# Spread tables in steps behind the mode products, the first pair's x w behind the last unit, and Y's first rows built pair by pair, in a windowed attention with a Fourier mixing layer

## The chip, the cores and the metric

The kernel runs on one core of one Trainium2 chip. The metric is the device time of one execution in microseconds; 433.08 us is the median of three runs of the kernel before (432.17 to 433.22). Times inside an execution count from the start of the profiled span.

## The reference

Eight batches, eight heads, 576 positions, head width 64. Attention looks back over 64 positions; its output, heads side by side, is x (8 x 576 x 512). Then, over the sequence:

```
X  = rfft(x, axis=1)                     # only the first 64 modes are used
Yr = Xr @ w_r[m] - Xi @ w_i[m]           # per mode m: a 512 x 512 matrix pair
Yi = Xr @ w_i[m] + Xi @ w_r[m]
y  = irfft(Y, n=576);  u = x + y
out = u + relu(u @ w_ch)
```

The 64 modes' two matrices are 128 MiB in float32 and are read once. The kernel splits u @ w_ch into x @ w_ch and y @ w_ch, and computes the latter as (inverse transform) @ (Y @ w_ch).

## The kernel before, in words

**First part (0 to about 190 us).** Attention and forward transform, while GpSimd (POOL) already issues loads of mode matrices, cast to bf16 on the way. Modes are taken in 16 groups of four. The first ten groups (`EARLY`) need their weights in two halves of the input channels: the first halves are used during attention, the second ones right after it.

**Second part.** The loop at L1048 walks over the remaining entries of `steps`. Each entry has two halves, `ri` 0 and 1, which use one load of `w_r` and one of `w_i`, each 1024 KB as it lands. Twenty halves finish the first ten groups with `mode_half` (L198); then 24 halves do the six other groups with `mode_pair` (L216), two modes at a time. One half is: 8 or 16 small matmuls with the weights of one load as the moving operand; `load_weights`, which has POOL issue the next load as soon as a buffer is free; whatever `ready` holds (mostly the turn of the last result by four matmuls, L694 or L722); and some calls of `advance`, paced by `want` (L1096 to L1104). Of `steps[20:]` all loads go to the three buffers of `ringA`, so a load can only be issued once the half that used the buffer's old content has been computed. The instruction order of every engine is the program's order.

`advance` works off a list of jobs with a delay of one: it prepares a job and finishes the one before. The first jobs are x @ w_ch for 36 tiles of 128 rows: four transposes (L639), an ACT copy (L614), four float32 matmuls into a bank (`multiply`, L646), a DVE copy to `XW` (L856). Ten of these (`NX0`) go beside the first twenty halves.

**The boundary** (`i == EARLY`, L1051): the jobs are drained, memory of the first stage is closed, Zall and the second XW pool are opened, part of Yall is cleared, and `spread_tables` (L768) runs. It makes, from the inverse transform's tables `trigI` (bf16) and `trigIr` (float32), copies whose rows are spread to the row order of the last two groups' results (`trigL`, `trigX`, `trigLr`, `trigXr`). For each of the two tables DVE clears a scratch tile and copies identity columns into it (L775, L777), TensorE multiplies (L782, L786, L789: six matmuls), and ACT copies four results out of PSUM (L790 to L792). One table's scratch is a `stg` tile, the other's a `tr` tile. The results are first used behind the loop, at L900 and L907.

**The last units.** Groups 12 and 13 (`LAST`, `LAST + 1`) come last, as four pairs of modes, i = 0 to 3. When group 15 is complete, the batch jobs start: for each batch the first 112 rows of Y are turned, multiplied with `w_ch` (`Zall`), and used for the output tiles (`early_u` L806, `add_late` L796), as many calls of `advance` as the pacing puts behind each of the eight last halves. Before the half before last all jobs are finished. Before the very last half (L1068) three `put_first` (L727; they gather the pairs' results, transposed, as rows of Y into a bank `late["first"]` of pool `z`) and `tail_xw(0)` (L890: XW of the first two output tiles into PSUM) are issued. `tail_xw` uses a float32 identity, `put_first` two matmuls of 256 columns.

**The end** (L1108 on): pair 3's `turn`, `put_first`, `take` (ACT and DVE copies into `trz`, L733); YL copied from `first`, L1115; the last rows' product with `w_ch`, L1119, in a bank of pool `y` and one of pool `z`; then for each pair of output tiles the low-rank products (L900, L907), additions and the store by SP. PSUM has eight banks: pools `m`, `t` and `z` with two each, `y` and `p` with one each. A bank is only written again when its last content has been read.

Of the kernel before, what the change touches and what calls it, by code (L numbers as in the profile page):

```python
# [9 lines left out]
FP32 = mybir.dt.float32  # L10
FP32R = mybir.dt.float32r
# [15 lines left out]
def kernel(  # L27
# [196 lines left out]
    with tc.manual_schedule():  # L224
# [480 lines left out]
        def finish_pair(grp, h, psm):  # L705
            if h == 0:
                late["stg"] = stgpool.tile([128, DM], BF16, name="stg")
            stg = late["stg"][:, HALF * h:HALF * h + HALF]
            nc.vector.tensor_copy(out=stg, in_=psm[:, 0:HALF])
            i = 2 * (grp % 2) + h  # L710
            end = grp - grp % 2 == LAST
            if i == (1 if end else 0):
                late["pt"] = bank("p", [128, NDCH, 128])
            other = bank("m", [128, NDCH, 128]) if end and i == 3 else None

            def pts(half):
                return other if half and other else late["pt"]

            def turn():
                for c in range(NDCH):  # L720
                    half = c // 2
                    nc.tensor.matmul(out=pts(half)[:, c, 32 * i:32 * i + 32], lhsT=stg[:, 128 * (c % 2):128 * (c % 2) + 128],  # L722
                                     rhs=lateT[:, half] if end else sel[:, half::2], start=True, stop=True)

            def put_first():
                for half in range(2):
                    nc.tensor.matmul(out=late["first"][:, HALF * half:HALF * half + HALF],  # L727
                                     lhsT=pick[:, half, 88 - 8 * i:216 - 8 * i], rhs=stg,
                                     start=(i == half == 0), stop=(i == 3), skip_group_check=True)

            def take():
                for by, cs in ((nc.scalar.copy, slice(0, 2)), (nc.vector.tensor_copy, slice(2, 4))):
                    by(out=trz[:, cs, :, 8 * i:8 * i + 8],  # L733
                       in_=pts(cs.start // 2)[:, cs, 32 * i:32 * i + 32].rearrange("p c (g x) -> p c g x", x=8))

            def prepare():
                turn()
                if end:
                    take()
                elif i == 3:  # L740
                    give_rows(grp, late["pt"])

            if end:
                late[i] = turn, put_first, take
            if end and i == 0:
                late["held"] = prepare
            elif not (end and i == 3):
                if end and i == 1:
                    ready.append(late["held"])
                ready.append(prepare)  # L750
# [14 lines left out]

            jobs.append((prepare, done))

        def spread_tables():  # L768
            for table, wide, two, one, spread in (
                    (trigI, trigL, trigX, ident_bf, stgpool.tile([128, DM], BF16, name="stg")),  # L770
                    (trigIr, trigLr, trigXr, ident_r,
                     trpool.tile([128, NDCH, 128], FP32R, name="tr").rearrange("p c k -> p (c k)"))):
                spread = spread[:, 0:256].rearrange("p (x g k y) -> p x g k y", x=2, g=4, y=2)
                plain = spread if table is trigI else spread.bitcast(FP32)
                nc.vector.memset(plain.rearrange("p x g k y -> p (x g k y)"), 0.0)  # L775
                for x in range(2):
                    nc.vector.tensor_copy(out=spread[:, x, :, :, x],  # L777
                                          in_=one[:, rows].unsqueeze(1).to_broadcast([128, 4, 16]))
                pt = bank("y")
                for x in range(2):  # L780
                    lhsT = spread[:, x].rearrange("p g k y -> p (g k y)")
                    nc.tensor.matmul(out=pt[:, 0:128], lhsT=lhsT, rhs=table[:, S - 64 + 64 * x:S + 64 + 64 * x],  # L782
                                     start=(x == 0), stop=(x == 1))
                for x in range(2):
                    lhsT = spread[:, x].rearrange("p g k y -> p (g k y)")
                    nc.tensor.matmul(out=pt[:, 128 + 64 * x:192 + 64 * x], lhsT=lhsT, rhs=table[:, 512:S],  # L786
                                     start=True, stop=True, skip_group_check=True)
                    pw = bank("z")
                    nc.tensor.matmul(out=pw, lhsT=lhsT, rhs=table[:, 0:512], start=True, stop=True)  # L789
                    nc.scalar.copy(out=wide[:, x, 0:512], in_=pw)  # L790
                nc.scalar.copy(out=two, in_=pt[:, 0:128])
                nc.scalar.copy(out=wide[:, :, 512:S], in_=pt[:, 128:256].rearrange("p (x k) -> p x k", x=2))  # L792

        UE = {}

# [187 lines left out]

        def new_ut():
            nonlocal taken_uts
            if not homes:
                homes.append(utpool.tile([128, 2, DM], FP32, name="utx"))
            elif taken_uts == len(homes) < NUT:
                t = ringA.tile([128, 4, DM], FP32, name="ut", tag="wt")
                homes.extend([t[:, 0:2], t[:, 2:4]])  # L990
            taken_uts += 1
            return homes[(taken_uts - 1) % NUT]
# [51 lines left out]
        NX0 = 10  # L1044
        x_jobs(pool("xp0", reuse_waits="tile"), 0, NX0)
        half = given = 0
        n0, n1 = 2 * EARLY, 4 * (NGRP - EARLY)
        for i, (grp, hb) in enumerate(steps[EARLY:]):  # L1048
            if i == 2:
                whole_modes()  # L1050
            if i == EARLY:  # L1051
                while tables:
                    tables.pop(0)()
                while jobs or pend:
                    advance()
                close(stmp2, yp, ringB)
                Zall = pool("zall", side="right").tile([2 * NM, B, DM], FP32R, name="Zall")
                x_jobs(pool("xp1", side="right", reuse_waits="tile"), NX0, NT)
                utpool = pool("utpool", side="right", reuse_waits="tile")
                nc.vector.memset(YT[:, :, :, rows], 0.0)  # L1060
                spread_tables()
                given = 0
            psm = bank("m")
            for ri in range(2):
                if half == n0 + n1 - 2:
                    while jobs or pend:
                        advance()
                if half == n0 + n1 - 1:  # L1068
                    late["first"] = bank("z")
                    for pair in range(3):  # L1070
                        late[pair][1]()
                    tail_xw(0)
                (mode_half if grp < EARLY else mode_pair)(psm, EARLY + i, ri)
                load_weights(len(wlist))
                while ready:
                    ready.pop(0)()
                for t in tables[0:2]:
                    t()
                del tables[0:2]
                if half == 0:  # L1080
                    nc.gpsimd.dma_start(out=wch, in_=moe_w_ch.rearrange("(c p) e -> p c e", p=128))
                if ri:
                    if grp < EARLY:
                        finish_group(grp, psm)
                    else:
                        finish_pair(grp, hb, psm)
                    if (grp, hb) == (NGRP - 1, 1):
                        ready.pop(0)()
                        for b in range(B):
                            batch_job(b)  # L1090
                            if 0 < b <= NLB:
                                early_jobs(b - 1)
                            if b % 2:
                                add_late(9 * (b // 2) + 8)
                half += 1
                if half <= n0:  # L1096
                    want = max(half - 4, 0) * NX0 // (n0 - 4)
                elif half <= n0 + n1 - 8:
                    want = (half - n0) * (NT - NX0) // (n1 - 8)
                else:  # L1100
                    want = NT - NX0 + (half - n0 - n1 + 8) * (B + 7 * NLB + 4) * 2 // 11
                while given < want:
                    advance()
                    given += 1  # L1104
# [2 lines left out]

        turn, put_first, take = late[3]  # L1108
        first = late["first"]
        turn()  # L1110
        put_first()
        ZL = trpool.tile([128, NDCH, 128], FP32R, name="tr").rearrange("p c k -> p (c k)")
        YL = stgpool.tile([128, DM], BF16, name="stg")
        take()
        nc.vector.tensor_copy(out=YL, in_=first)  # L1115
        zl = [bank("y"), bank("z")]
        for h, ps_ in enumerate(zl):
            for c in range(NDCH):
                nc.tensor.matmul(out=ps_[:, 0:HALF], lhsT=trz[:, c].rearrange("p g k -> p (g k)"),  # L1119
# [55 lines left out]
```

## Time and profile before

| | |
|---|---|
| median of three runs | 433.08 us (432.17 to 433.22) |
| the profiled execution | 433.11 us, of which the span is 431.1 us (2.0 us lie around it) |
| TensorE (PE) matmuls | 330.0 us busy, 77% of the span |
| VectorE (DVE) / ScalarE (ACT) / GpSimd (POOL) | 238.6 / 182.9 / 103.8 us |
| DMA | 93.28 MB by the page's count of packets, mean 216 GB/s; HBM read 163.58 MB |
| mean granted TensorE clock | 0.905 |
| the chain that ended last | DMA 55%, PE 28%, issue 7%, DVE 5% |

Busy times of engines overlap, so they do not add up to the span. The chain of waits says which of them set the end: up to 361 us mostly transfers of `w_r` and `w_i`, after that PE with DVE. GB/s in the profile counts what the DMA engines write; a load of 1024 KB at 213 GB/s takes 4.9 us. A timeline line gives start, duration, engine, line, operation, operands, count, and in brackets how long the engine was idle before it and what ended that. PEld is the loading of the stationary operand, which runs beside PE.

### The profile page before, as it was taken

Reading aid. Unit: us, or ns where it says so; the run is one execution under the profiler, and the core shown is the slowest. Engines: PE = TensorE matmul, PEld = TensorE weight load, DVE = VectorE, ACT = ScalarE, POOL = GpSimd, SP = SyncE. Lnnn points to the kernel's source line nnn. Section 1 sums busy time; section 2 is a strip of 40 time slices with the busy share of each in tenths; the row PEclk is TensorE's granted clock in tenths of the full one; section 3 lists DMA queues with packets and bytes.
Section 4 is the critical chain, followed back from the end, with each engine's and each line's share of the span. In section 5 each row is a group of like instructions: output and inputs, shape, how many; then the busy total and the mean of one; then the engine's idle time right before and its main releaser. Section 6 shows DMA issues by size and latency. Waiting matters only on the chain.

```text
span 431.1 us, 11458 instructions
## 1 busy us (share of the span) xinstructions
PE 330.0 (77%) x5006; PEld 218.2 (51%) x5006; DVE 238.6 (55%) x509; ACT 182.9 (42%) x330; POOL 103.8 (24%) x153
## 2 busy tenths in 40 slices
PE   6999999999999999973307344676575668979994
PEld 3666767576677667651104122444453445535552
DVE  7688787877776766866104111123222224874995
ACT  5665757566666656532201101142121213433663
POOL 8322223222131231112112100011111111120894
PEclk8899999999999999988557768569999989999999
DMA  8999999999999999999999999989999999995698
GB/s 203 211 211 212 212 211 212 211 211 212 211 213 211 212 212 211 212 212 212 211 258 212 212 211 212 215 173 212 215 215 214 214 214 214 215 214 113 223 364 310
DMA packets 40819, 93.28 MB, mean 216 GB/s; under 512 B 2529, under 2 KB 2785, under 8 KB 40769
## 3 DMA queue, kind: packets, MB, share of 16 engines
q0 software_dynamic: 35056, 81.80, 98.4%
q1 hardware_dynamic: 5568, 10.62, 6.7%
q8 instruction: 39, 0.64, 0.5%
q10 hardware_dynamic: 144, 0.13, 0.1%
q14 instruction: 12, 0.09, 0.1%
HBM read 163.58 MB, written 9.44 MB: 401 GB/s over the span
## 4 chain that ended last, share of the span: by engine, by line
DMA 55%; PE 28%; issue 7%; DVE 5%; ACT 2%; POOL 2%; DVEq 0%; POOLq 0%
DMA wr<-in_moe_w_r_dram 34%; DMA wi<-in_moe_w_i_dram 12%; DMA rawk<-in_k_dram 7%; PE tr L260 4%; PE s L307 3%; PE psz L646 2%; PE s L319 2%; PE s L299 2%; PE pt L327 2%; PE vb L272 2%; DVE xw L802 2%; PE psm L198 1%; PE psm L216 1%; PE o L347 1%; DMA vd<-in_k_dram 1%
## 5 line engine op out<-in xcount | busy, mean ns | idle before, releaser
L646 PE MATMUL psz<-wch,tr 128*128 128x512 f32 x176 | 59.2, 466 | 11.4 <-DMA wch<-in_moe_w_ch_dram 10.9
L856 DVE CAST xw<-psz 128x512 fp32r<-128x512 f32 x36 | 24.9, 692 | 73.6 <-PE psz L646 73.1
L311 DVE TENSOR_REDUCE mx<-s 128x4 fp32r<-128x512 f32 x72 | 49.5, 688 | 24.2 <-PE s L307 23.9
L614 ACT CAST tr<-ptx 128x512 fp32r<-128x512 bf16 x36 | 21.2, 588 | 95.4 <-PE ptx L639 95.4
L321 ACT ACTIVATE p<-s 128x512 bf16<-128x512 f32 x72 | 39.7, 602 | 13.0 <-PE s L319 13.0
L646 PEld LDWEIGHTS psz<-wch,tr 128*128 128x128 f32 x176 | 35.1, 221 | 18.7 <-issue 11.3
L198 PEld LDWEIGHTS <-XQ 128*32 128x32 bf16 x320 | 13.0, 175 | 45.5 <-issue 27.3
L264 ACT COPY kT<-tr 128x576 bf16<-128x576 bf16 x32 | 23.2, 725 | 22.8 <-PE tr L260 22.8
L198 PE MATMUL psm<-wi,XQ 128*32 128x512 bf16 x144 | 14.8, 486 | 20.6 <-DMA wi<-in_moe_w_i_dram 20.6
L307 PE MATMUL s<-kT,qT 64*64 64x128 bf16 (+1 forms) x576 | 29.2, 221 | 0.0
L299 PE MATMUL s<-mask_t,ident_bf 128*128 128x512 bf16 x72 | 28.4, 395 | 0.6
L330 DVE COPY pts<-pt 128x1024 bf16<-128x1024 bf16 (+1 forms) x40 | 25.2, 630 | 5.3 <-PE pt L327 3.8
L264 ACT COPY qT<-tr 128x576 bf16<-128x576 bf16 x32 | 23.3, 727 | 9.8 <-PE tr L260 9.8
L686 DVE TENSOR_TENSOR stg<-psm,Yfour 128x512 bf16<-128x512 f32 x10 | 6.9, 690 | 36.4 <-PE psm L198 33.5
L178 POOL DMA_DIRECT2D wi<-in_moe_w_i_dram x18 | 13.7, 758 | 55.3 <-PE psm L198 35.5
L307 PEld LDWEIGHTS <-qT 64*64 64x64 bf16 x576 | 18.0, 107 | 17.7 <-issue 17.2
L319 PE MATMUL s<-mx,ident_r 128*128 128x512 f32 x72 | 26.2, 437 | 0.0
L169 POOL DMA_DIRECT2D wr<-in_moe_w_r_dram x12 | 8.4, 698 | 69.8 <-PE psm L216 33.3
L264 ACT COPY vT<-tr 128x576 bf16<-128x576 bf16 x32 | 23.3, 728 | 4.0 <-PE tr L260 3.9
L198 PE MATMUL psm<-wr,XQ 128*32 128x512 bf16 x120 | 11.9, 478 | 16.3 <-DMA wr<-in_moe_w_r_dram 15.7
L327 PE MATMUL pt<-ident_bf,p 128*128 128x128 bf16 x288 | 23.3, 220 | 0.9 <-issue 0.8
L216 PEld LDWEIGHTS <-XQ 128*32 128x32 bf16 x256 | 9.2, 151 | 29.3 <-issue 29.2
(259 smaller groups left out, 672.2 us busy)
## 6 DMA issues: line engine op xcount, KB each, us to landing
wi<-in_moe_w_i_dram POOLq DMA_DIRECT2D x29, 1024.0 KB, 19.1
wr<-in_moe_w_r_dram POOLq DMA_DIRECT2D x27, 1024.0 KB, 19.2
out_dram<-ut SPq DMA_DIRECT2D x29, 256.0 KB, 2.8
rawv<-in_v_dram POOLq DMA_DIRECT2D x16, 288.0 KB, 16.0
rawk<-in_k_dram POOLq DMA_DIRECT2D x15, 288.0 KB, 15.1
rawq<-in_q_dram POOLq DMA_DIRECT2D x15, 288.0 KB, 15.0
x_sb<-in_moe_w_r_dram POOLq DMA_DIRECT2D x2, 1024.0 KB, 15.9
out_dram<-utx SPq DMA_DIRECT2D x6, 256.0 KB, 2.6
```

Source lines behind the costliest of these rows:

```text
L198: nc.tensor.matmul(out=psm[32 * g:32 * g + 32, :], lhsT=XQ[hb].rearrange("k s b m -> k (s b) m")[:, (3 * j + 1 - ri) * B:(3 * j + 5 - ri) ...
L264: nc.scalar.copy(out=to, in_=pt.rearrange("p j n -> p n j"))
L299: nc.tensor.matmul(out=s, lhsT=ident_bf, rhs=mask_t[:, mk], start=True, stop=True)
L307: nc.tensor.matmul(out=s[ro, t, lo:128], lhsT=lq, rhs=kT[ro, 64 * n - 64 + lo:64 * n + 64], start=False, stop=True, skip_group_check=True)
L311: nc.vector.tensor_reduce(out=mx, in_=s, axis=AX.X, op=ALU.max, negate=True)
L319: nc.tensor.matmul(out=s, lhsT=ident_r, rhs=mx.unsqueeze(2).to_broadcast([128, 4, 128]), start=False, stop=True, skip_group_check=True)
L321: nc.scalar.activation(out=p[:, 4 * c2:4 * c2 + 4, :], in_=s, func=ACT_F.Exp, scale=EX_SCALE)
L327: nc.tensor.transpose(out=pt[:, t, :], in_=st[u]["p"][:, t, :], identity=ident_bf)
L330: nc.vector.tensor_copy(out=ps[:, 0:nt, :], in_=pt[:, 0:nt, :])
L614: nc.scalar.copy(out=tr, in_=pt)
L646: nc.tensor.matmul(out=pz, lhsT=tr[:, c, :], rhs=wch[:, c, :], start=(c == 0), stop=(c == NDCH - 1))
L856: nc.vector.tensor_copy(out=XW[i], in_=multiply(tr))
```

## The change

Three things move; nothing is computed that was not computed before.

1. `spread_tables` becomes `spread_steps`, three functions: `clear` (all DVE work of both tables) and one `multiply_by` for each table (its six matmuls and four ACT copies). From the second half behind the boundary on, one of them runs per half, behind the half's products and `ready`. The scratch is the first output tile `utx`, which is now taken at the boundary, and `trz`. The jobs are no longer drained at the boundary, so the tenth x @ w_ch product comes one half later.
2. `put_first` is called inside each pair's `prepare`, behind its `turn`, and its bank comes from pool `y`, taken with pair 1. The two banks of the last rows' product both come from pool `z`.
3. `tail_xw(0)` moves from before the last half to behind the loop, just before pair 3's `turn`.

```diff
             if i == (1 if end else 0):
                 late["pt"] = bank("p", [128, NDCH, 128])
+                if end:
+                    late["first"] = bank("y")
...
                 turn()
                 if end:
+                    put_first()
                     take()
...
-        def spread_tables():
-            for table, wide, two, one, spread in (
...
+        def spread_steps(scratch):
+            flat = scratch.rearrange("p j e -> p (j e)")[:, 0:128]
+            flat_r = trz.rearrange("p c g k -> p (c g k)")[:, 0:256]
+            todo = ((trigI, trigL, trigX, ident_bf, flat.bitcast(BF16), flat),
+                    (trigIr, trigLr, trigXr, ident_r, flat_r, flat_r.bitcast(FP32)))
...
+            def clear():
+                for table, wide, two, one, spread, plain in todo:
+                    nc.vector.memset(plain, 0.0)
+                    for x in range(2):
+                        nc.vector.tensor_copy(out=lanes(spread)[:, x, :, :, x],
+                                              in_=one[:, rows].unsqueeze(1).to_broadcast([128, 4, 16]))
+
+            def multiply_by(table, wide, two, one, spread, plain):
                 pt = bank("y")
...
+            return [clear] + [lambda t=t: multiply_by(*t) for t in todo]
...
-                while jobs or pend:
-                    advance()
                 close(stmp2, yp, ringB)
...
                 nc.vector.memset(YT[:, :, :, rows], 0.0)
-                spread_tables()
+                homes.append(utpool.tile([128, 2, DM], FP32, name="utx"))
+                spread = spread_steps(homes[0])
...
-                if half == n0 + n1 - 1:
-                    late["first"] = bank("z")
-                    for pair in range(3):
-                        late[pair][1]()
-                    tail_xw(0)
                 (mode_half if grp < EARLY else mode_pair)(psm, EARLY + i, ri)
                 load_weights(len(wlist))
                 while ready:
                     ready.pop(0)()
+                if spread and half > n0:
+                    spread.pop(0)()
...
         first = late["first"]
+        tail_xw(0)
         turn()
         put_first()
...
-        zl = [bank("y"), bank("z")]
+        zl = [bank("z"), bank("z")]
```

`n0` is 20, the number of the first stage's halves; `half` counts all of them, 0 to 43.

More of the change, by code (lines that the diff above doesn't have):

```diff
@@ L766, in batch_job, with lanes @@
             jobs.append((prepare, done))
-        def spread_tables():
-            for table, wide, two, one, spread in (
[L770 to L778, printed above, removed]
+        def spread_steps(scratch):
[3 more added lines that the diff above has]
+                    (trigIr, trigLr, trigXr, ident_r, flat_r, flat_r.bitcast(FP32)))
+            def lanes(spread):
+                return spread.rearrange("p (x g k y) -> p x g k y", x=2, g=4, y=2)
+            def clear():
[5 more added lines that the diff above has]
+            def multiply_by(table, wide, two, one, spread, plain):
                 pt = bank("y")
                 for x in range(2):
-                    lhsT = spread[:, x].rearrange("p g k y -> p (g k y)")
+                    lhsT = spread[:, 128 * x:128 * x + 128]
                     nc.tensor.matmul(out=pt[:, 0:128], lhsT=lhsT, rhs=table[:, S - 64 + 64 * x:S + 64 + 64 * x],
@@ L784, in spread_tables @@
                 for x in range(2):
-                    lhsT = spread[:, x].rearrange("p g k y -> p (g k y)")
+                    lhsT = spread[:, 128 * x:128 * x + 128]
                     nc.tensor.matmul(out=pt[:, 128 + 64 * x:192 + 64 * x], lhsT=lhsT, rhs=table[:, 512:S],
@@ L985, in new_ut @@
             nonlocal taken_uts
-            if not homes:
-                homes.append(utpool.tile([128, 2, DM], FP32, name="utx"))
-            elif taken_uts == len(homes) < NUT:
+            if taken_uts == len(homes) < NUT:
                 t = ringA.tile([128, 4, DM], FP32, name="ut", tag="wt")
@@ L1046 @@
         half = given = 0
+        spread = []
         n0, n1 = 2 * EARLY, 4 * (NGRP - EARLY)
```

## The prediction

> **What bounds the kernel now.** I read the chain of waits first. From 243 us it consists of transfers of `w_r` and `w_i` with a 0.7 us group of PE products behind each, until 361.05 us; from there it runs through PE and DVE to the end. So a microsecond won before 361 us counts only if a transfer lands earlier, and one won behind it counts if PE or DVE on that chain gets it. The change touches both parts: the tables at 278 to 288 us, the order around the last unit at 394 to 398 us.
>
> For the first place I read the stretches of two microseconds (columns: window, its length, then busy time and count of PE, PEld, DVE, ACT, POOL, granted clock, DMA share, GB/s):
>
> ```profile
> 284.00:286.00 2.00, 1.14 (x4) 1.14 (x5) 0.00 (x0) 0.81 (x3) 0.00 (x0) 0.50 1.02 205
> 286.00:288.00 2.00, 2.00 (x22) 1.02 (x21) 0.00 (x0) 1.51 (x4) 0.00 (x0) 0.50 0.62 125
> 288.00:290.00 2.00, 2.00 (x28) 1.35 (x28) 0.23 (x1) 1.07 (x2) 0.71 (x1) 0.50 0.63 117
> 290.00:292.00 2.00, 2.00 (x13) 1.55 (x11) 0.59 (x2) 0.69 (x2) 0.70 (x1) 0.79 0.97 172
> 292.00:294.00 2.00, 2.00 (x30) 1.38 (x29) 0.99 (x2) 0.57 (x2) 0.30 (x1) 1.00 1.07 215
> ```
>
> DMA has a hole just behind the tables: against 213 GB/s it lacks 88, 96 and 41 GB/s for 2 us each, 450 KB, worth 450 / 213 = 2.1 us. The timeline shows the cause:
>
> ```profile
> 276.67 1.12 PE L198 MATMUL psm<-wi,XQ 128*32 128x512 bf16 x8 [1.27 <-DMA wi<-in_moe_w_i_dram]
> 278.08 3.26 PE L646 MATMUL psz<-wch,tr 128*128 128x512 f32 x8
> 282.78 0.33 PE L782 MATMUL psy<-trigI,stg 128*128 128x128 bf16 x2 [1.44 <-DVE stg L777]
> 284.86 0.69 PE L782 MATMUL psy<-trigIr,tr 128*128 128x128 f32 x2 [1.26 <-ACT trigL L792]
> 286.86 1.08 PE L216 MATMUL psm<-wr,XQ 128*32 128x256 bf16 x16
> 288.26 0.71 POOL L169 DMA_DIRECT2D wi<-in_moe_w_i_dram  x1 [9.48 <-PE psm L216]
> 296.25 0.67 PE L216 MATMUL psm<-wi,XQ 128*32 128x256 bf16 x16 [1.44 <-DMA wi<-in_moe_w_i_dram]
> 301.94 0.67 PE L216 MATMUL psm<-wr,XQ 128*32 128x256 bf16 x16 [2.49 <-DMA wr<-in_moe_w_r_dram]
> ```
>
> The first L216 starts at 286.86 behind the tables and waits for no DMA; POOL waited 9.48 us for it before it could issue the next load. The trace's completion marks (sixteen per load, one for each DMA engine) give that L216's load as landed at 281.58: it ran 5.3 us late.
>
> **Is the hole on the path?** The second thing to see: products that wait for their load start at 242.06 and, seven loads on, at 276.67, 4.94 us per load; from 276.67 to 296.25 four loads, 4.90 us each. Across the hole no landing is late. The sixteen marks say why. Of the load that landed at 281.58 eight came at 276.4 to 277.5 and eight at 280.7 to 281.6; of the one at 291.31 eight at 286.2 to 287.3 and eight at 290.4 to 291.3; of the one at 296.20 all at 295.4 to 296.2. Eight engines run up to 5 us ahead of the others, and the hole is their idle time. The late eight were busy until 290.4 to 291.3, and the load issued at 288.26 was there for them (296.20 - 291.31 = 4.89, one full pace). Products wait for the last mark, so filling the hole gives the early eight their lead back and moves no landing. The Trainium skill, "DMA: Bandwidth & Descriptors", section "Why a DMA increments its semaphore by 16 and not by 1", says that the engines of one transfer finish independently and only the full count means landed; these marks agree.
>
> **The change, part by part.**
>
> *Tables.* Removed from before the first L216: one product of four matmuls, the tables' twelve matmuls (0.83 us from 282.78 and 2.08 us from 284.86) and their waits for DVE and ACT. L216 can start at its landing, 281.6; POOL issues the next load at about 283.0 instead of 288.26; SP has no issue near. Value by the marks 0; ends 0 and -2.1 (the whole hole as time).
>
> *Where the tables go.* By the instruction order they stand behind the products of the third and fourth half (landings about 291.3 and 296.2). Each adds to its half at most 0.83 or 2.08 us of PE, plus waits for two pool-`z` banks emptied by ACT (1.07 + 0.28 + 0.30 = 1.65 us, and 1.78 us, of ACT); queued behind are only that half's transposes and x @ w_ch products. The cover is PE's wait for loads: 24.0 us in 12 halves from 296 to 356 us, 2.0 each. Value 0. Without cover at most 0.83 + 1.65 + 2.08 + 1.78 = 6.3 us; but L216 was 5.3 us late before without a late landing, so nearly all of that is absorbed even then. `clear` is the same six DVE instructions, DVE idles 7 of 10 there: 0. The job that is no longer drained is one product a half later; the pacing ends in the same state: 0. `utx` and `trz` are not used until 383 us: 0.
>
> *`put_first` pair by pair.* Pairs 0 and 1 give four matmuls to the stretch at 383 us, about 0.1 us each by their weight loads (six in 0.56). Two lie inside PE's wait of 0.56 us for DVE at 383.61. The other two push L815 from 383.71 to about 383.9; the addition L821 stands on DVE behind a copy that ends at 384.36 anyway. Value 0, ends 0 and +0.2. Its bank `y` was last read near 374.7, and the next use of `y` is L900: 0.
>
> *Last unit.* The stretch that sets the end:
>
> ```profile
> 394.45 0.69 PE L216 MATMUL psm<-wr,XL 128*32 128x256 bf16 x16
> 395.06 0.17 PEld L722 LDWEIGHTS <-stg 128*128 128x128 bf16 x4 [0.17 <-issue]
> 395.15 0.56 PEld L727 LDWEIGHTS <-pick 128*128 128x128 bf16 x6
> 395.72 0.30 PEld L890 LDWEIGHTS pst<-xw,ident_r 128*128 128x128 f32 x2
> 396.39 0.69 PE L216 MATMUL psm<-wi,XL 128*32 128x256 bf16 x16
> 397.15 0.42 DVE L709 CAST stg<-psm 128x256 bf16<-128x256 f32 x1 [1.32 <-PE psm L216]
> 397.63 0.21 PE L722 MATMUL psp<-pick,stg 128*128 128x32 bf16 x2 [0.56 <-DVE stg L709]
> ```
>
> Here the chain has PE at 394.45, then the last L216, the cast, the turn. After the change only two of six L727 stand before the last L216: 395.15 + 0.19, then the 0.17 to 0.25 gap that PEld shows before a new group: L216 at 395.55, against 396.39, 0.8 earlier. Its last load has its last mark at 395.30, so 0.25 us of room is left. The cast then ends at 396.75. Meanwhile L890 takes its 0.67 us (395.72 to 396.39) behind L216's weights (395.55 + 0.44): done at 396.8 with a gap of 0.15, at 397.0 with the 0.36 that stands before L216 here. PE was idle 0.56 us in that place. The turn starts at 396.8 to 397.05 instead of 397.63: 0.6 to 0.8 gained, 0.8 taken, because the short gap belongs to bf16 groups before. Behind it the same instructions follow; YL's bank `y` is free once L1115 has read it, where L900 before waited for L663; both `z` banks are read by the same copies: 0 (ends -0.2 and +0.2).
>
> **Sum.** 0 + 0 + 0 - 0.8 on the profiled execution's 433.11 us (span 431.1, 2.0 around it) gives 432.3; that execution lies 0.03 above the median, so the forecast for the median is **432.3**. About 0.3% (1.3 us: 431.8 to 434.4) is what a measurement of this kernel can tell from no change.
>
> **Rivals.**
>
> *The hole is time.* If the early engines' lead is worth something (they take over what delays the late ones), landings move by up to 2.1 us and everything from 296 to 394 us follows, since PE waits for loads up to 361.05. For it: the page's 173 GB/s in that slice. Against: four landings on pace. 433.1 - 2.1 - 0.8 = 430.2, though the last marks must move with it. The Trainium skill's fit for one transfer, in "DMA: Bandwidth & Descriptors", section "Anatomy of one DMA — SWDGE (gpsimd) path", makes time a fixed part plus bytes over a rate; read that way, missing bytes are missing time. The marks speak against that reading.
>
> *One late landing goes.* The load at 301.94 came 5.69 us behind the one before, 0.8 over the pace; fifteen marks came by 301.16, one at 301.90, and a 16 KB packet of queue q8 (0.94 us) ran at 296.48. If after the change an early engine carries this, landings move 0.8: 431.5.
>
> *Nothing on the last unit.* L890 now stands between the last L216 and the turn; if it costs its 0.71 us there in full, or the last load's marks end later, the gain is near 0: 433.0.
>
> *Slower: PE falls behind the loads at the tables.* Place: second to fifth half, 286 to 307 us. The clock was 0.50 from 284 to 290 us; if, with PE now waiting for loads between groups, it stays there, rows of this clock give: second half L216 1.08 + two jobs of 0.61 + 2.06 = 6.4 us, third 1.08 + 0.39 + 0.83 + 2.67 = 5.0, fourth 1.08 + 2.08 + 5.34 = 8.5, fifth 1.08 + 0.39 + 5.34 = 6.8, end to end from 286.5 to 313.2, where the sixth half starts 6.4 us behind its load of 306.8. With all of ACT's 1.65 and 1.78 us as waits it is 9.8. It decides above the 5.3 us that were harmless: 1.1 to 4.5 us of missing landings, 2.8 in the middle, less 0.8: 435.1. Against it: PE is busy without a pause from 286.5 on in this case, and before such a stretch brought the full clock within the window from 290 us (0.79). The Trainium skill, "TensorE: Matmul & The Clock Gate", section "What's actually happening", states that activity releases a halved clock; it would end this rival after some microseconds, as at 290 us.
>
> **How the numbers follow.** Forecast 432.3: 0.49. Hole 430.2: 0.18. One landing 431.5: 0.10. Nothing gained 433.0: 0.10. Slower 435.1: 0.13. Faster by over 0.3%: 0.18 + 0.10 = 0.28. Within: 0.49 + 0.10 = 0.59. Slower: 0.13. The range 430.1 to 434.0 takes in the hole's end and leaves out the slower case; the forecast's own is 431.8 to 432.8.
>
> **What would show it.** After the change: no window under 200 GB/s between 284 and 294 us, the first L216 at about 281.6 and the next load issued near 283; yet the products at about 296.2, 301.9 and 361.0 unmoved. The last L216 at about 1.9 us behind the start of the one before it becomes 1.1; the last turn comes 2.4 us behind it instead of 3.2. If the product at 361.0 comes at 359, the marks misled me; if L216 falls over 5 us behind its landing after 291 us, the slower rival holds.

## The result, and the profile after

| | before | after |
|---|---|---|
| median (executions) | 432.98 us (432.17 to 435.62; 19) | 432.07 us (431.46 to 432.49; 19) |
| profiled execution, its span | 433.11, 431.1 us | 432.25, 430.4 us |
| mean granted TensorE clock | 0.905 | 0.886 |
| DMA and PE in the chain that ended last | 55%, 28% | 49%, 37% |

The ratio after to before is 0.9975 (95% interval 0.9963 to 0.9986), 1.1 us of 433. The forecast was 432.3 us, 0.8 below the profiled execution of before; the profiled execution of after is 0.86 below it. The chain of waits follows loads until 376.24 us now (361.05 before); what comes behind is PE with ACT and DVE, as before.

First the stretches behind the boundary in the kernel after (columns as in the prediction: window, length, busy time and count of PE, PEld, DVE, ACT, POOL, granted clock, DMA share, GB/s):

```profile
284.00:286.00 2.00, 1.20 (x3) 0.53 (x3) 0.76 (x2) 0.07 (x1) 0.00 (x0) 0.50 1.06 213
286.00:288.00 2.00, 1.56 (x21) 1.16 (x21) 1.37 (x7) 0.00 (x0) 0.16 (x1) 0.50 1.07 215
288.00:290.00 2.00, 2.00 (x8) 1.28 (x8) 0.08 (x2) 0.59 (x1) 0.54 (x1) 0.50 1.08 219
290.00:292.00 2.00, 2.00 (x20) 1.44 (x21) 0.85 (x2) 0.59 (x1) 0.00 (x0) 0.73 1.05 211
292.00:294.00 2.00, 1.79 (x28) 1.17 (x21) 0.45 (x1) 1.08 (x3) 0.71 (x1) 1.00 1.06 215
```

The hole is gone: no window is under 211 GB/s, where before had 125, 117 and 172. The clock is at half until the fourth window, as before, and then full. The timeline of the same stretch, in after:

```profile
281.55 1.09 PE L216 MATMUL psm<-wr,XQ 128*32 128x256 bf16 x16 [1.49 <-DMA wr<-in_moe_w_r_dram]
282.95 0.71 POOL L169 DMA_DIRECT2D wi<-in_moe_w_i_dram  x1 [4.23 <-PE psm L216]
286.44 1.09 PE L216 MATMUL psm<-wi,XQ 128*32 128x256 bf16 x16 [1.24 <-DMA wi<-in_moe_w_i_dram]
291.65 0.67 PE L216 MATMUL psm<-wr,XQ 128*32 128x256 bf16 x16
292.37 0.27 PE L791 MATMUL psy<-trigI,utx 128*128 128x128 bf16 x2
296.18 0.67 PE L216 MATMUL psm<-wi,XQ 128*32 128x256 bf16 x16 [1.42 <-DMA wi<-in_moe_w_i_dram]
296.78 0.44 PE L791 MATMUL psy<-trigIr,trz 128*128 128x128 f32 x2
301.96 0.67 PE L216 MATMUL psm<-wr,XQ 128*32 128x256 bf16 x16 [1.16 <-DMA wr<-in_moe_w_r_dram]
```

The first L216 waits for its load and starts at 281.55 (before 286.86), the next load is issued at 282.95 (before 288.26), 5.3 us earlier both. Yet the products at 296.18 and 301.96 stand where they stood (296.25 and 301.94): 5.3 us of earlier issue moved those landings by 0.07 us at most. The tables (L791) now stand behind the third and fourth half, and the half behind each still finds PE early enough.

Then the last unit of after:

```profile
394.41 0.68 PE L216 MATMUL psm<-wr,XL 128*32 128x256 bf16 x16
395.03 0.17 PEld L724 LDWEIGHTS <-stg 128*128 128x128 bf16 x4 [0.17 <-issue]
395.45 0.87 PE L216 MATMUL psm<-wi,XL 128*32 128x256 bf16 x16
396.25 0.30 PEld L901 LDWEIGHTS pst<-xw,ident_r 128*128 128x128 f32 x2 [0.17 <-issue]
396.36 0.42 DVE L709 CAST stg<-psm 128x256 bf16<-128x256 f32 x1 [0.55 <-PE psm L216]
396.83 0.17 PEld L724 LDWEIGHTS <-stg 128*128 128x128 bf16 x4 [0.29 <-DVE stg L709]
396.84 0.22 PE L724 MATMUL psp<-pick,stg 128*128 128x32 bf16 x2
```

The half before the last starts at 394.41, against 394.45 before. The last L216 now comes 1.04 us behind it (was 1.94), the cast begins at 396.36 instead of 397.15, the turn at 396.84 instead of 397.63. So the turn comes 0.79 us earlier; 0.04 of that was there at 394.41 already, and 0.75 arises in these two microseconds. The remaining 0.07 of the 0.86 us between the two profiled executions lies behind the turn or outside the span.

### The profile page after: what moved, and what is told of

Same layout as the page of the kernel before. It is cut to its first block, busy times and chain, and to the rows that moved or that the text cites. A ratio compares the mean times of both kernels' runs of the same rounds, so it can differ in the third digit from the quotient of the medians.

```text
span 430.4 us, 11413 instructions
## 1 busy us (share of the span) xinstructions
PE 328.2 (76%) x4962; PEld 220.9 (51%) x5006; DVE 239.5 (56%) x509; ACT 182.6 (42%) x330; POOL 103.4 (24%) x153
## 4 chain that ended last, share of the span: by engine, by line
DMA 49%; PE 37%; issue 6%; ACT 3%; DVE 3%; POOL 1%; DVEq 0%; POOLq 0%
DMA wi<-in_moe_w_i_dram 29%; DMA wr<-in_moe_w_r_dram 19%; PE tr L260 6%; PE s L307 4%; PE s L319 3%; PE pt L327 3%; PE vb L272 3%; PE o L347 2%; PE s L299 2%; PE psm L216 2%; PE psz L646 2%; PE psm L198 1%; PE pst L901 1%; DMA vd<-in_k_dram 1%; PE psz L901 1%
## 5 line engine op out<-in xcount | busy, mean ns | idle before, releaser
L646 PE MATMUL psz<-wch,tr 128*128 128x512 f32 x176 | 63.2, 490 | 11.7 <-DMA wch<-in_moe_w_ch_dram 10.9
L646 PEld LDWEIGHTS psz<-wch,tr 128*128 128x128 f32 x176 | 36.8, 232 | 19.6 <-issue 11.3
L247 POOL DMA_DIRECT2D rawk<-in_k_dram x15 | 8.1, 538 | 70.5 <-PE tr L260 64.2
L216 PEld LDWEIGHTS <-XQ 128*32 128x32 bf16 x256 | 9.4, 151 | 28.4 <-issue 26.0
```

The costliest lines, as they stand in the source:

```text
L646: nc.tensor.matmul(out=pz, lhsT=tr[:, c, :], rhs=wch[:, c, :], start=(c == 0), stop=(c == NDCH - 1))
```

## The experiments

**Theories.** Mine: the gain is the last unit's, about 0.8 us; the tables' place is worth nothing, because the hole was idle time of eight early DMA engines and the eight late ones set every landing. Rival one: the hole is time, and filling it gives up to 2.1 us. Rival two: the tables' lateness is harmless only up to an edge close by, so that their removal is worth something in part of the executions. "Before + ..." means the kernel before with that edit alone; medians are given with the number of executions, ratios against the kernel before on the same chip.

**Last unit alone** (twice, e1 and e9): parts 2 and 3 of the change, tables as before.

```diff
+                if end:
+                    late["first"] = bank("y")
...
                 if end:
+                    put_first()
                     take()
...
-                if half == n0 + n1 - 1:
-                    late["first"] = bank("z")
-                    for pair in range(3):
-                        late[pair][1]()
-                    tail_xw(0)
...
+        tail_xw(0)
         turn()
...
-        zl = [bank("y"), bank("z")]
+        zl = [bank("z"), bank("z")]
```

> The kernel before with the changes to the last unit alone (put_first pair by pair, x w behind the last unit); the tables stay in one piece at the boundary. If filling the hole in the DMA stream is worth nothing: all of the gain, 0.8 to 1.0 us under the kernel before, and the hole of 2.1 us stays in its trace. If the hole was time, even in part: less than the whole change gains, with the rest in the run with the tables alone.

Measured: 432.16 us (431.47 to 433.02; 12), ratio 0.9981 (0.9968 to 0.9993). Within the noise the gain is there without the tables. One thing expected was not found: in this profiled execution the hole is small (201 and 168 GB/s in the first two windows from 284 us, 221 in the third; the clock was 1.00 there, and the first L216 came at 284.00). So this profile alone does not show that a full hole is free; e9 repeats the kernel, beside the whole change and the tables alone.

> The changes to the last unit alone once more, tables in one piece at the boundary: 0.8 us under the kernel before in the median. If the place of the tables sits on an edge, its executions scatter wider upwards than those of the whole change, with one or two 1 to 3 us over the median; if not, the same scatter.

Measured: 432.21 us (431.72 to 432.59; 11), ratio 0.9983 (0.9975 to 0.9992). The scatter is that of the whole change (highest 432.59 here, 432.50 in e8), so by this expectation no edge shows in these eleven executions. This time the profiled execution had the hole in full; its windows:

```profile
284.00:286.00 2.00, 0.98 (x5) 0.75 (x4) 0.00 (x0) 1.20 (x4) 0.00 (x0) 0.50 0.96 193
286.00:288.00 2.00, 2.00 (x20) 1.29 (x19) 0.00 (x0) 1.22 (x3) 0.00 (x0) 0.50 0.57 115
288.00:290.00 2.00, 2.00 (x37) 1.37 (x30) 0.23 (x1) 1.37 (x4) 0.71 (x1) 0.71 0.50 100
290.00:292.00 2.00, 2.00 (x13) 1.37 (x12) 0.89 (x2) 1.18 (x2) 0.70 (x1) 1.00 0.82 104
```

Missing against 213 GB/s: (20 + 98 + 113 + 109) x 2 / 213 = 3.2 us, more than in before. One load landed 7.06 us behind the one before it, 2.2 over the pace of 4.9; the next came 4.26 behind, which gives 0.6 back (0.6 of the lateness was one engine's alone: the other fifteen marks had come by 297.26, the last at 297.89). That execution took 432.56 us, 0.44 more than the profiled one of e1 with a hole of 0.5 us. Six times the hole goes with under half a microsecond at the end, in the same kernel; but these are two single executions out of a scatter from 431.5 to 433.0 us, so the 0.44 is a hint and no price.

**Tables alone** (twice, e2 and e10): before + part 1 of the change, drain included.

```diff
-                while jobs or pend:
-                    advance()
...
-                spread_tables()
+                homes.append(utpool.tile([128, 2, DM], FP32, name="utx"))
+                spread = spread_steps(homes[0])
...
+                if spread and half > n0:
+                    spread.pop(0)()
```

> The kernel before with the tables in three steps and without the drain at the boundary; the last unit as before. If the late eight DMA engines set the landings: within 0.3 us of the kernel before, although no window from 284 to 294 us falls under 200 GB/s. If missing bytes are missing time: up to 2.1 us faster. If PE falls behind at the tables: slower by 0.5 us or more.

Measured: 432.56 us (432.26 to 433.42; 12), ratio 0.9990 (0.9975 to 1.0004).

> The tables in steps alone once more: 0 to 0.3 us under the kernel before in the median, none of its executions above 434, where the kernel before has had some. If the tables are worth a constant amount: 0.3 us or more in the median.

Measured: 432.83 us (432.43 to 433.68; 12), ratio 0.9992 (0.9977 to 1.0006). In both profiles the hole is gone and the first L216 stands at its landing (281.62 and 281.51). Both intervals contain 1 and exclude the 2.1 us (0.9952) of the first rival, which falls. None of e10's executions is over 434 us, as expected. A value of 0.4 us (0.09%, the middle of both ratios) can be neither shown nor excluded, and the intervals reach to 1.1 us; by the medians alone the tables give 0.23 us (e2, before 432.79) and 0.06 us (e10, before 432.89).

**The whole change again** (e8), on the chip of e9 and e10.

> The whole change once more, on the same chip as the next two. If the tables' place costs nothing in most executions and 2 us in a few (the kernel with x w alone behind the last unit showed one such execution): median within 0.2 us of the last unit alone, highest execution below 433. If the tables are worth a constant 0.3 us or more: median lower than the last unit alone by that.

Measured: 432.21 us (431.30 to 432.50; 11), ratio 0.9979 (0.9971 to 0.9988): the same median as the last unit alone.

**The halves of the last unit.** e3 has the `put_first` pair by pair and keeps `tail_xw(0)` before the last half; e4 moves only that line.

```diff
+                if end:
+                    late["first"] = bank("y")
...
                 if end:
+                    put_first()
                     take()
...
                 if half == n0 + n1 - 1:
-                    late["first"] = bank("z")
-                    for pair in range(3):
-                        late[pair][1]()
                     tail_xw(0)
...
-        zl = [bank("y"), bank("z")]
+        zl = [bank("z"), bank("z")]
```

> The kernel before with put_first pair by pair alone; x w stays before the last half. Four of six matmuls of 0.1 us each leave the place before the last unit, so its products start 0.4 us earlier: 0.4 us faster if nothing else ends late there. If the last load's mark ends the wait instead, less than 0.2.

Measured: 432.62 us (431.68 to 433.01; 12), ratio 0.9989 (0.9976 to 1.0003). The last L216 comes 1.51 us behind the half before it.

```diff
                 if half == n0 + n1 - 1:
...
-                    tail_xw(0)
...
+        tail_xw(0)
         turn()
```

> The kernel before with x w behind the last unit alone; three put_first stay together before the last half. x w holds PE for 0.67 us there and PE is idle for 0.56 us behind the last unit: 0.5 to 0.67 us faster if it fits into that idle time. If x w then delays the turn by all that it takes, or the last load ends late, under 0.2. Together with the run of put_first alone it should come to more than the 0.8 to 1.0 of both, if the last load's end cuts the sum.

Measured: 432.39 us (431.66 to 434.03; 12), ratio 0.9985 (0.9971 to 1.0). The last L216 comes 1.48 us behind. In the traces, where the whole change has 1.04 and before 1.94, each half of the edit takes off 0.43 or 0.46, and 0.43 + 0.46 = 0.89 is the 0.90 of both. In time, 0.11% + 0.15% = 0.26% against the 0.17 to 0.19% of both together: the direction is that of a cut by something else at the end, but the intervals do not separate them. What cuts is shown by e1's own last unit:

```profile
394.94 0.66 PE L216 MATMUL psm<-wi,XL 128*32 128x256 bf16 x12
395.80 0.44 PE L216 MATMUL psm<-wi,XL 128*32 128x256 bf16 x4 [0.20 <-DMA wi<-in_moe_w_i_dram]
396.16 0.30 PEld L893 LDWEIGHTS pst<-xw,ident_r 128*128 128x128 f32 x2 [0.17 <-issue]
396.27 0.42 DVE L709 CAST stg<-psm 128x256 bf16<-128x256 f32 x1 [0.98 <-PE psm L216]
```

The last group splits: twelve matmuls run, then PE waits for the last part of the last load (fifteen of its marks came by 394.99, the sixteenth at 395.75). In the kernel before, these products did not wait for that load; with about 0.9 us of PE's work ahead of them gone, they do. e8 shows the same (group at 395.08, 1.17 us long, last mark at 395.77).

e4's profiled execution, 434.03 us, also shows what the second rival asks for. Its boundary is that of before to the hundredth, and its next landing is not:

```profile
286.86 1.08 PE L216 MATMUL psm<-wr,XQ 128*32 128x256 bf16 x16
288.26 0.71 POOL L169 DMA_DIRECT2D wi<-in_moe_w_i_dram  x1 [9.49 <-PE psm L216]
298.27 1.09 PE L216 MATMUL psm<-wi,XQ 128*32 128x256 bf16 x16 [3.42 <-DMA wi<-in_moe_w_i_dram]
```

298.27 instead of 296.25: the load issued at 288.26 landed 6.9 us behind the one before it. Fifteen of its sixteen marks came by 296.98, most of them by 296.2, and the last at 298.23. In this execution the hole sat on the path, by 2.0 us. From 290 to 292.5 us the mean DMA share was 0.94, against 1.00 in before, about 2.4 us of one of sixteen engines (0.06 x 2.5 x 16): as far as this shows, a late engine had nothing to do. Why it got its part of the load later than in before, with the same time of issue, stays open.

**How far is the edge?** e5 calls `spread_tables()` twice; e6 makes only the bf16 table once more. Both repeat work whose result is the same.

```diff
                 spread_tables()
+                spread_tables()
```

> The kernel before with the tables made twice at the boundary, so that the first products behind it start 4.8 us later again (about 10 us behind their load's landing instead of 5.3). If lateness is free until the late eight DMA engines run out of work: the next load is issued at about 293.0 instead of 288.3, begins about 2.3 us later, 4.0 us after the late engines became free at 291.3, and the time rises by 4 us. If lateness of any size is paid for: 4.8 us. If there is slack up to 361 us that takes it in: under 1 us.

Measured: 437.11 us (436.25 to 438.87; 4), ratio 1.0095 (1.0061 to 1.0129), 4.1 us. Its timeline:

```profile
289.82 1.08 PE L216 MATMUL psm<-wr,XQ 128*32 128x256 bf16 x16
291.23 0.71 POOL L169 DMA_DIRECT2D wi<-in_moe_w_i_dram  x1 [13.67 <-PE psm L216]
```

The first L216 runs 9.1 us behind its landing (280.76), and the load issued at 291.23 lands at 300.50, 10.0 behind the one before it: 5.1 over the pace. Of these, 1.2 are one engine's alone: the other fifteen marks came by 299.31, 3.9 over the pace. In time the interval, 2.6 to 5.6 us, rules out the third case (slack, under 1 us), and does not separate 4 from 4.8 us.

```diff
-        def spread_tables():
+        def spread_tables(n=2):
...
+                spread_tables(1)
                 spread_tables()
```

> The kernel before with the bf16 table alone made once more at the boundary: 2.5 us later (about 7.8 us behind the landing). Free until the late engines run out: the next load is issued at about 290.8, begins at about 293.1, 1.8 us after 291.3, and the time rises by 1.8 us, clearly less than the 2.5 us of the delay. Every delay paid: 2.5 us. Mean over sixteen engines counts: 1.3 us for half of the delay and more.

Measured: 434.30 us (432.97 to 436.29; 10), ratio 1.0024 (1.0006 to 1.0042), 1.0 us, with a wide scatter.

```profile
286.98 1.08 PE L216 MATMUL psm<-wr,XQ 128*32 128x256 bf16 x16
288.38 0.71 POOL L169 DMA_DIRECT2D wi<-in_moe_w_i_dram  x1 [10.22 <-PE psm L216]
296.99 0.67 PE L216 MATMUL psm<-wi,XQ 128*32 128x256 bf16 x16 [1.64 <-DMA wi<-in_moe_w_i_dram]
```

Here the first L216 ran only 5.7 us behind its landing (281.29), not the 7.8 that I had reckoned with, and 0.1 us later than in before; so this profile tells none of the three expected cases from the others. The next landing (296.95) was 1.0 over the pace.

All profiled executions side by side show more than one at a time (e7 is left out, since it adds PE work in most halves):

| kernel | tables | first L216 behind its landing | next landing behind the one before it | half before the last starts | cast comes behind that |
|---|---|---|---|---|---|
| before | in one piece | 5.3 | 4.89 | 394.45 | 2.70 |
| e4 | in one piece | 5.3 | 6.93 | 395.84 | 2.25 |
| e6 | in one piece, the bf16 one twice | 5.7 | 5.91 | 394.89 | 2.71 |
| e9 | in one piece | 6.2 | 7.06 | 394.94 | 1.80 |
| e5 | in one piece, twice | 9.1 | 10.00 | 397.56 | 2.71 |
| e1 | in one piece | 2.7 | 4.90 | 393.90 | 2.37 |
| e3 | in one piece | 4.1 | 4.90 | 393.91 | 2.28 |
| after | in steps | 0.0 | 4.89 | 394.41 | 1.95 |
| e8 | in steps | 0.0 | 4.90 | 394.04 | 2.24 |
| e2 | in steps | 0.0 | 4.96 | 393.65 | 2.71 |
| e10 | in steps | 0.1 | 4.89 | 394.27 | 2.71 |

The last column depends on the edit of the last unit only: 2.70 or 2.71 without it, 1.80 to 2.37 with all of it, 2.25 and 2.28 with one half. The third and fourth columns show the edge: up to 4.1 us of lateness the next landing is on pace; at 5.3 us it is on pace once (before) and 2.0 late once (e4); 5.7, 6.2 and 9.1 us go with 1.0, 2.2 and 5.1. The fifth column speaks against a hole that is always free: the five executions in which the first L216 was 5.3 us late or more reach the half before the last at 394.45 to 397.56, the six others at 393.65 to 394.41. But these are single executions, the nearest two of them 0.04 us apart, and before's later start may come from 301.90, a landing 0.8 us over the pace. A like landing in after (301.92), e8 and e10 was partly made up by the next (4.26, 4.56 and 4.25 us behind it); in before it was not (4.87).

The times of all executions give a hint of the same. Of 102 executions of the kernel before, nine took more than 434 us; of 54 with the tables in steps (after, e2, e8, e10) none did (highest 433.68); of 47 with the tables in one piece and the last unit changed in whole or in part (e1, e3, e4, e9) one did, which is few for a place on an edge. So the second rival holds in single executions; in the median little of it is left.

**More PE instructions** (e7): after, with 28 small matmuls more in each of 36 halves, into a bank that nobody reads. They are no part of the computation.

```diff
                 load_weights(len(wlist))
+                if half < 36:
+                    spare_bank = bank("y")
+                    for _ in range(28):
+                        nc.tensor.matmul(out=spare_bank[0:32, 0:32], lhsT=ident_bf[:, 0:32], rhs=ident_bf[:, 0:32],
+                                         start=True, stop=True, tile_position=(0, 0))
```

> The changed kernel with 28 small matmuls more (32 rows, 32 columns, 2 PE instructions each) in each of 36 halves, into a bank that nobody reads: 2016 PE instructions, about 1 us of PE per half, where PE waits about 2 us for its load. If the packets of queue q8 (16 KB, 0.94 us of one DMA engine each, 39 of them) bring PE's instructions and make the late eight engines late: about eight such packets more between 190 and 355 us, one on each late engine, landings 0.7 to 0.95 us later by 355 us, time 0.6 to 1.0 us up. If the late engines are late for another reason and PE has the room: no change within 0.3 us.

Measured: 433.15 us (432.68 to 434.07; 10), ratio to before 0.9998 (0.9982 to 1.0013), about 1.0 us over after's 0.9975. The page's list of DMA queues in after:

```profile
q8 instruction: 39, 0.64, 0.5%
```

39 packets, 0.64 MB together, about 16 KB each. e7 has 47: eight more for 2016 more PE instructions, 252 each, as 10,012 instructions of PE (half of them weight loads) / 39 = 257 in before. From 277 to 357 us the landings took 79.66 us instead of 78.80, 0.86 more; but PE itself ran late there (L216 at 358.70 behind a landing at 356.76), so which of the two the 1.0 us is made of stays open.

## Why the prediction was right, point by point

*What bounds the kernel.* Right: until 376 us loads, then PE with ACT and DVE. Of the 5.3 us won in POOL's issue, 0.04 us is left at the half before the last in these two executions (394.41 against 394.45).

*Tables' removal, value 0 between 0 and -2.1.* Right in the median as far as the noise lets one tell, with too good an opinion of its safety. The early eight engines keep their lead in after (marks 5.4 to 4.0 us ahead of the last one in the load that landed at 296.13) and the last marks did not move. But the step took "the load issued at 288.26 was there for them" as if there were room; e4, e9 and e6 show that there was almost none. In the profiled executions a full hole went with 0 to 2.2 us at the next landing, and with a start of the half before the last that is later than in every other one of the table. What this adds to the median is small, but not shown to be nothing: e2 and e10 put it at about 0.4 us, with intervals from a loss of 0.3 us to a gain of 1.1.

*Tables in the third and fourth half, value 0.* Right: 296.18, 301.96, and the wait of 1.16 us before the latter show cover left. PE's waits for loads from 296 to 356 us fell from 24.0 to 19.3 us.

*"Unmoved" at 361.0.* A miss of size: the product came at 360.71, 0.34 earlier, and between 306 and 361 us landings were 0.35 to 0.72 us earlier. The load at 301.92 was still 5.79 behind the one before, as in the forecast, but the next came only 4.26 behind, so part of the late landing was given back. In size that comes near the rival in which one late landing goes (0.8 us), but the late landing did not go; the one behind it caught up, and the runs do not show by what. By 394 us the lead was gone: 376.24 is a landing 5.84 us behind the one before it, and from there PE's own work sets the pace (394.41 against 394.45).

*`put_first` for pairs 0 and 1, value 0.* Right: from the half at 382.10 to that at 388.03 it is 5.93 us (5.87 before), to 394.41 6.38 (6.40 before): +0.06 and -0.02.

*Last unit, -0.8.* Right in sum (0.75 in these two microseconds), with two terms off that nearly cancel. The last L216 came 1.04 behind the half before it (forecast 1.1), so it started 0.1 earlier than reckoned. Mis-sized was "0.25 us of room": the last load's last mark came at 395.84 in after (395.77 in e8), not at 395.30, so the last L216 took 0.87 us instead of 0.69. Between executions the last mark of this load differs by 0.5 us, more than the room that I read from one of them. The Trainium skill, "DMA: Bandwidth & Descriptors", section "Why a DMA increments its semaphore by 16 and not by 1", says that the engines of one transfer finish independently of each other. The marks of this load agree: in e1 fifteen had come by 394.99 and the last came at 395.75. The turn came 2.43 behind the half before the last (forecast 2.4). That one execution met the forecast so closely is in part luck: by the last column of the table the same edit took off 0.90 us in e9, but 0.46 in e8 and 0.33 in e1, where PE waited for the last load within the group.

*x w behind the last L216.* Right, and as close as the forecast had it: its weights load at 396.25, beside the cast, and the turn's weights at 396.83 wait for the cast (396.36 + 0.42 = 396.78) and not for x w. The rival in which it costs 0.7 us there did not happen.

*Slower rival.* Did not happen: with the clock at half until 291 us PE was 0.4 us late at one half (291.65 behind a landing at 291.24) and on time at the next.

What is open: how often the hole reaches the path, since landings can be seen only in profiled executions, one for each kernel; and how much of the 1.1 us the tables' place is worth, 0 or the 0.4 us that e2 and e10 cannot exclude. The last unit alone (0.8 and 0.7 us by its two ratios) is the larger part either way.

## What to carry to other kernels

A dip in DMA throughput is not yet lost time: look at the last completion mark of each load on both sides of it, and count only what those marks lost. But one execution does not show that a lateness is harmless: here 5.3 us were free at the next landing in one profile and cost 2.0 us in another. And where PE's chain and the last load end within half a microsecond of each other, a cut of one of them is paid out only as far as the other.

## What the runs showed of the hardware

- The sixteen DMA engines of one stream of loads drift apart: eight ran 4 to 5 us, one load, ahead of the others for tens of microseconds. A full hole behind the tables levels them (from one load to the next the spread of the marks falls from 5.1 to 0.8 us in before, from 5.4 to 1.9 in e9); the hole of 0.5 us in e1 does not (5.6 to 3.9).
- Packets of q8 come one for every 255 or so PE instructions and take 0.88 to 0.98 us of one DMA engine (nine packets from 190 to 400 us in before). One of them moved a late mark by about 1.0 us (before: from 1.97 to 0.91 us ahead of the last, at the packet of 275.3); a landing such as that of 301.92, 0.9 us over the pace with fifteen marks in by 301.09, looks like one that struck the last engine.
- The clock at one place differs between executions of kernels with the same code there: 0.50 from 284 to 288 us in before and e9, 1.00 in e1 and e3. The first L216 behind the tables came at 286.86 and 287.26 us in the former, at 284.00 and 285.37 in the latter.
